# Attention's last DVE and ACT steps laid out anew, gathers tied to layer 1 in every slot, and a branch hint for PE read from a flag

## Chip, cores and metric

One core of one Trainium2 chip. The metric is the device time of one execution in microseconds, the median of the runs shown. Lower is better. TensorE is called PE in the profile, VectorE DVE, ScalarE ACT, GpSimd POOL, SyncE SP.

## What is computed

Sigmoid attention for 8 batches, 12 heads, 448 tokens of 64 values, then a mixture of 8 experts over the 3584 tokens of 768 values. Each token goes to the one expert with the largest gate logit; that expert's two layers are run on it and the result is scaled.

```python
scores = q @ k.T / sqrt(64) - log(448)
x = sigmoid(scores) @ v                      # per head; heads side by side: (3584, 768)
logits = x @ w_gate
e = argmax(logits, 1)
gate_w = softmax(logits)[e]                  # with 1e-9 in the denominator
eom = sigmoid(x @ w_output_gate)[e]
for each expert e:                           # w1: 768 x 1024, w2: 1024 x 768
    out[its tokens] = gate_w * eom * (relu(x[its tokens] @ w1[e]) @ w2[e])
```

Matmuls of the experts run as three passes on operands split in a rounded part and a rest (fp32r), which is what split() makes: a cast on ACT for the high part and a subtract on DVE for the low part.

## The kernel before

**Attention** is a loop over 168 units (L661) and two more that drain it. Seven units make a group of two head pairs, three groups make a batch. A unit issues, in this order: loads of q and k (i == 0), unit(u - 168), the routing step "places" (i == 1), scores(u), values(u - 2), the gate matmuls of the batch before (i == 3 of a batch's first group), loads of v, the routing steps "logits" (i == 6) and "counts" (i == 0), and scatters of list rows. Every engine works its own queue strictly in this order. scores (L582) are eight matmuls on PE and one sigmoid on ACT, into one of two PSUM pairs; values (L592) are eight matmuls on PE and, at i of 2, 3 and 6, the copies, adds and transposes of DVE that take a result out of PSUM (an eviction set: L600 or L604, L610, L611).

**Routing** (route, L198) is done per batch in four steps: logits (L206 to L212), counts (three sigmoids on ACT, L221 to L228 on DVE), places (L230 to L240), rows (scatters by POOL into the lists of the experts). find_run and early_table (L269) work out on DVE which expert a slot takes.

**unit(u)** (L686) counts u up to 0 at attention's end and starts the first two expert slots ahead of time, while attention still runs: early_table for slots 0 and 1, loads of the six w1 rows of slot 0 by SP (load_w) and their splits (split_w1_row, L410), list loads and copies (early_list), the gathers of slot 0's tokens by POOL (gather_rows), their transposes on DVE (turn_rows, L427) and their splits (split_rows, L433). A cast of a split stands in ACT's queue ahead of the unit's sigmoid, since unit() comes before scores().

**Slots** (slot, L504): an expert with up to 448 tokens (14 gathers of 32) or 256 tokens (8). Layer 1 is eight steps f of 18 matmuls, with a relu on ACT and a subtract on DVE for each; layer 2 is up to six blocks of 24 matmuls and, with 448 tokens, two blocks of 16 in layer2_rest (L488) after the second. Layer 2 takes three PSUM buffers in turn. Meanwhile the slot gathers the tokens of the next one (xg), turns them (turn_x) and splits them (split_x) when layer 1 is done, and loads and splits the next weights. side() is a generator that is stepped once in each f and each block of slots 0 and 1: the last batch's routing, late_table, then in turns a load of lists by SP and copies of lists by POOL (spread_lists, L364 to L367). In slot 0 (begun) two gathers are issued in each f of 0 to 6 and wait for layer 1's matmul or relu (paced); in the others all gathers are issued at the slot's start and wait for nothing of layer 1.

**Branches**: slots from the third late one on stand in nested Ifs (L783 to L787) on a register, full; then come slots of 256 tokens in nested Ifs on part (L790). Behind an If that isn't taken every engine steps its semaphore up to the count that it would have had. With these inputs five late slots of 448 tokens run, three of them inside the Ifs, and two of 256.

Of the kernel before, what the change touches and what calls it, by code (L numbers as in the profile page):

```python
# [12 lines left out]
ALU = mybir.AluOpType  # L13
# [41 lines left out]
class Kernel:  # L55
# [233 lines left out]
    def late_table(self):  # L289
        v, t = self.nc.vector, self.scratch_tiles()  # L290
        tt = v.tensor_tensor
        n = LATE_N
        keep = lambda nm, shape: self.const.tile(shape, I32, name=nm)
        sl = self.slots[:, :, 0:n].unsqueeze(3).broadcast_to([1, 2, n, E])
        left, first = t([1, E]), t([1, n])
        pos, tab = t([1, n, E]), t([1, 3, n])
        cmp, num, end = t([1, E, KT]), t([1, 2, E]), t([1, 2, E])
        base, sel = t([1, 2, E]), t([1, 2, E])
        bc = lambda a: a.unsqueeze(1).broadcast_to([1, n, E])
        self.find_run()  # L300
        tt(left, self.run, self.taken, ALU.subtract)
        tt(cmp, left.unsqueeze(2).broadcast_to([1, E, KT]), self.kts.unsqueeze(1).broadcast_to([1, E, KT]), ALU.is_gt)
        v.tensor_reduce(num[:, 0], cmp, AX.X, ALU.add)
        v.tensor_tensor_scan(end[:, 0], self.one8, num[:, 0], 0.0, ALU.mult, ALU.add)
        tt(base[:, 0], end[:, 0], num[:, 0], ALU.subtract)
        tt(sel[:, 0], self.taken, self.ebase, ALU.add)
        v.scalar_tensor_tensor(sel[:, 1], num[:, 0], float(TB), sel[:, 0], ALU.mult, ALU.add)
        v.scalar_tensor_tensor(num[:, 1], num[:, 0], float(TB), left, ALU.mult, ALU.is_lt)
        v.scalar_tensor_tensor(sel[:, 0], base[:, 0], -float(TB), sel[:, 0], ALU.mult, ALU.add)
        v.tensor_tensor_scan(end[:, 1], self.one8, num[:, 1], 0.0, ALU.mult, ALU.add)  # L310
        tt(base[:, 1], end[:, 1], num[:, 1], ALU.subtract)
        yield 1
        ohb, tb, tmb = t([1, E, E]), t([1, 3, E]), t([1, E, E])
        bb = lambda a: a.unsqueeze(1).broadcast_to([1, E, E])
        slb = self.slots[:, 0, 0:E].unsqueeze(2).broadcast_to([1, E, E])
        tt(ohb, slb, bb(base[:, 1]), ALU.is_ge)
        tt(tmb, slb, bb(end[:, 1]), ALU.is_ge)
        tt(ohb, ohb, tmb, ALU.subtract)
        tt(tmb, ohb, bb(self.ids), ALU.mult)
        v.tensor_reduce(tb[:, 0], tmb, AX.X, ALU.add)  # L320
        tt(tmb, ohb, bb(sel[:, 1]), ALU.mult)
        v.tensor_reduce(tb[:, 1], tmb, AX.X, ALU.add)
        v.tensor_reduce(tb[:, 2], ohb, AX.X, ALU.add)
        yield 1
        oh, tmp = t([1, n, E]), t([1, n, E])
        tt(oh, sl[:, 0], bc(base[:, 0]), ALU.is_ge)
        tt(tmp, sl[:, 0], bc(end[:, 0]), ALU.is_ge)
        tt(oh, oh, tmp, ALU.subtract)
        tt(tmp, oh, bc(self.ids), ALU.mult)
        v.tensor_reduce(tab[:, 0], tmp, AX.X, ALU.add)  # L330
        tt(pos, sl[:, 1], bc(sel[:, 0]), ALU.add)
        yield 1
        tt(pos, pos, oh, ALU.mult)
        v.tensor_reduce(tab[:, 1], pos, AX.X, ALU.add)
        v.tensor_reduce(tab[:, 2], oh, AX.X, ALU.add)
        v.tensor_scalar(first, self.slots[:, 0, 0:n], end[:, 0, E - 1:E], 0.0, ALU.is_equal, ALU.add)
        for i in range(3):
            v.scalar_tensor_tensor(tab[:, i], first, tb[:, i, 0:1], tab[:, i], ALU.mult, ALU.add)
        yield 1
        self.tab_l, self.tab_b, self.tot = keep("tabl", [1, 3, n]), keep("tabb", [1, 3, E]), keep("tot", [1, 2])  # L340
        v.tensor_copy(self.tab_l, tab)
        v.tensor_copy(self.tot, end[:, :, E - 1])
        v.tensor_copy(self.tab_b, tb)
        yield 1

    def take(self, key, tiles):
# [26 lines left out]
    def gather_rows(self, s, g, rows, pace=None):  # L373
# [1 line left out]
        self.paced(self.nc.gpsimd.indirect_dma_start(  # L375
            out=self.xg[:, g], out_offset=None, in_=x4,
            in_offset=bass.IndirectOffsetOnAxis(ap=s["lx"][:, g:g + 1], axis=0)), pace)

    def gather(self, s, rows=NT):
        for g in range(s["lx"].shape[1]):  # L380
            self.gather_rows(s, g, rows)

    def paced(self, i, pace):
        if pace is not None:
# [119 lines left out]
    def slot(self, cur, nxt, side=None, begun=False, hint=None):  # L504
        nx = None
        if nxt is not None:
            nx, rows, sure = nxt() if callable(nxt) else nxt
            if not begun:
                self.gather(nx, rows)
            if not sure:  # L510
                self.nc.gpsimd.drain()
        n = 32 * cur["lx"].shape[1]
        for f in range(8):
            self.layer1(f, n, begun and f == 0)
            if begun and f < 7:
                self.gather_rows(nx, 2 * f, rows, 1)
                self.gather_rows(nx, 2 * f + 1, rows, 0)
            if side is not None:
                next(side, None)
            if 1 <= f < 5:  # L520
                self.split_w2(f - 1)
                if f > 1:
                    self.load_w1(nx, f - 2)
        for k in range(3):
            self.turn_x(nx, k)
        self.split_x(nx, 0)
        self.split_x(nx, 1)
        for i in range(2 * (n // 128)):
            t = i // 2
            if hint is not None and i == 5:  # L530
                self.tc.mark_branch_hint_location(hint[0], hint=hint[1])
            self.layer2(cur, t, i % 2, self.ys[(t + (t > 0 and n % 128 > 0)) % 2])
            if i == 0:
                self.split_x(nx, 2)
            if i < 3 and nx is not None:
                self.split_w1(i)
                for k in range(i, 4 if i == 2 else i + 1):
                    self.load_w2(nx, k)
            if side is not None:
                next(side, None)  # L540
            if i == 1 and n % 128:
                self.layer2_rest(cur)
        return nx

    def attention(self, pool):
# [74 lines left out]
        def routing(at, u):  # L620
            if routes and want[0] == at:
                want[0] = next(routes[0])
                if want[0] == "rows":
                    first = u + 2 if len(rows) != B - 3 else U * NG - 20
                    rows.append((first, routes.pop(0)))
                    if routes:
                        want[0] = next(routes[0])
# [33 lines left out]
        for u in range(U * NG + LAG):  # L661
            g, i = divmod(u, U)
            if i == 0 and 0 < g < NG - 2:
                load_qk(g + 2)
            self.unit(u - U * NG)
            if i == 1:
                routing("places", u)
            if u < U * NG:
                scores(u)
            if u >= LAG:  # L670
                values(u - LAG)
            if i == 3 and g and g % GB == 0:
                gates(g // GB - 1)
            if i == 1 and 0 < g < NG - 2:
                load_v(g + 2)
            for r, name in ((6, "logits"), (0, "counts")):
                if i == r:
                    routing(name, u)
            scatters(u)
            if u == 10:  # L680
                self.init_list()
# [2 lines left out]
        return routes[-1]  # L684

    def unit(self, u):  # L686
        if u == -52:
            self.early_table(0)
            self.s0 = self.early_slot(0)
        if u == -32:  # L690
            self.early_table(1)
            self.s1 = self.early_slot(1)
        for k, a, b in ((0, -44, -42), (1, -12, -9)):
            if u == a:
                self.early_list(k, True)
            if u == b:
                self.early_list(k, False)
        for g in range(GB_):
            if u == -41 + (3 * g + 1) // 2:
                self.gather_rows(self.s0, g, ROWS_E[0], g % 2)  # L700
        for d in range(6):
            if u == (-46, -45, -43, -41, -35, -30)[d]:
                self.load_w(self.s0, self.w1, self.w1r, d, 1, 0)
            if u == (-36, -33, -30, -28, -22, -20)[d]:
                self.split_w1_row(d)
        for rows, a, b in (((0, 5), -26, -25), ((5, 10), -18, -17), ((10, GB_), -12, -11)):
            if u == a:
                self.turn_rows(self.s0, *rows)
            if u == b:
# [14 lines left out]
    def build(self, phases="abc"):  # L724
# [58 lines left out]
        with ExitStack() as ctx:  # L783
            for k in range(LATE_MIN, LATE_MAX):
                ctx.enter_context(tc.If(full > k, label=f"big{k}"))
                with tc.manual_schedule():
                    cur = self.slot(cur, late(k + 1), hint=(f"big{k + 1}", full > k + 1) if k + 1 < LATE_MAX else None)  # L787
        mid = lambda k: lambda: (self.slot_regs(self.tab_b, k, self.ltb[:, k], self.lxb[:, k], False), NT, False)
        lists = lambda k: dict(lt=self.ltb[:, k], lx=self.lxb[:, k])
        with ExitStack() as ctx:  # L790
# [39 lines left out]
```

## Time and profile before

| | before |
|---|---|
| median of 3 runs (lowest to highest) | 784.25 us (783.76 to 784.53) |
| the profiled execution | 792.04 us, its span 790.2 us |
| mean granted clock of PE in it | 0.988 |
| PE busy | 769.1 us, 97% |
| DVE busy | 398.4 us, 50% |
| ACT busy | 374.8 us, 47% |
| POOL busy | 261.7 us, 33% |

Attention takes the span from 0 to 285 us, the two early slots follow until 407.7, the five late slots of 448 tokens until 711, the two of 256 tokens until 783; then the last scatter lands. The profile is one execution, so its parts are read against its own span. Busy time is a mean over all stages: where PE has 97% over the span, it is the few stretches with less that can change. A queue's idle time carries what ended it in brackets.

### The profile page before, as it was taken

To read this page: it belongs to the slowest core of one execution; us is meant where nothing else is said; L and a number is where in the kernel's file an instruction comes from. 1 tells how busy PE (TensorE), PEld (TensorE's weight loads), DVE (VectorE), ACT (ScalarE), POOL (GpSimd) and SP (SyncE) were. 2 spreads that over 40 slices of the span, in tenths; PEclk is the share of its full clock that TensorE was granted. 3 is DMA by queue.
4 is the path that set the end of the run, shared out by engine and by line. 5 is a ranking of instruction groups with operands and counts; after the bars stand their busy time and mean duration, and the time that the engine had idled before them with its cause. 6 is when DMAs were issued, how large, how long until landed. Compare 5 with 4: busy or idle time off the path is not lost. (4 is left out here: it accounts for less than half of the span.)

```text
span 790.2 us, 14753 instructions
## 1 busy us (share of the span) xinstructions
PE 769.1 (97%) x5812; PEld 587.2 (74%) x5812; DVE 398.4 (50%) x712; ACT 374.8 (47%) x429; POOL 261.7 (33%) x374
## 2 busy tenths in 40 slices
PE   9999999999999899999999999999999999998996
PEld 4444444444333269999998999999999999998996
DVE  1373655737496549715614715615615524624564
ACT  5666666666567433424424424424424424424444
POOL 5011202112243326338736027017018117105161
PEclk9999999999999899999999999999999999999998
DMA  9475865757976355446354455254354354263541
GB/s 290 128 187 143 195 158 159 193 140 207 265 232 172 111 124 174 142 122 210 82 193 145 138 173 171 97 185 155 100 191 155 102 204 141 109 212 114 181 165 39
DMA packets 73462, 126.50 MB, mean 160 GB/s; under 512 B 15375, under 2 KB 53263, under 8 KB 73376
## 3 DMA queue, kind: packets, MB, share of 16 engines
q1 hardware_dynamic: 62768, 100.18, 42.5%
q0 software_dynamic: 9680, 24.53, 9.4%
q10 hardware_dynamic: 928, 0.69, 0.4%
q8 instruction: 49, 0.80, 0.4%
q14 instruction: 37, 0.30, 0.1%
HBM read 108.77 MB, written 23.09 MB: 167 GB/s over the span
## 5 line engine op out<-in xcount | busy, mean ns | idle before, releaser
L590 ACT ACTIVATE a<-ps,bias_s 128x896 f32<-128x896 f32 x168 | 169.0, 1008 | 92.9 <-PE ps L588 89.4
L588 PE MATMUL ps<-q,k 64*64 64x448 f32 x1344 | 161.7, 547 | 7.0 <-ACT a L590 7.0
L597 PE MATMUL ps<-a,v 64*64 64x448 f32 x1344 | 160.2, 543 | 0.7 <-DVE x L610 0.7
L449 PE MATMUL ps<-rounded 128*128 128x448 f32 (+1 forms) x432 | 151.7, 351 | 3.1 <-ACTq L783 2.8
L375 POOL DMA_INDIRECT plain<-x_dram,lxs x112 | 131.3, 1173 | 70.5 <-issue 26.7
L450 PE MATMUL ps<-rounded 128*128 128x448 f32 (+1 forms) x432 | 151.4, 350 | 0.7 <-issue 0.7
L451 PE MATMUL ps<-rounded 128*128 128x448 f32 (+1 forms) x432 | 151.3, 350 | 0.4 <-issue 0.4
L476 PE MATMUL ps<-w2h,h 128*128 128x384 f32 x400 | 133.6, 334 | 0.0
L478 PE MATMUL ps<-w2h,h 128*128 128x384 f32 x400 | 133.6, 334 | 0.0
L477 PE MATMUL ps<-w2l,h 128*128 128x384 f32 x400 | 133.6, 334 | 0.0
L462 DVE SCALAR_TENSOR_TENSOR h<-ps,h 128x384 fp32r<-128x384 f32 (+2 forms) x128 | 45.2, 390 | 165.4 <-ACT h L461 156.4
L405 DVE TENSOR_TENSOR rounded<-plain,rounded 128x2048 fp32r<-128x2048 f32 (+5 forms) x63 | 97.6, 1572 | 56.5 <-ACT rounded L404 56.4
L461 ACT ACTIVATE h<-ps 128x448 fp32r<-128x448 f32 (+1 forms) x72 | 36.8, 511 | 165.7 <-PE ps L451 132.9
L588 PEld LDWEIGHTS ps<-q,k 64*64 64x64 f32 x1344 | 51.7, 135 | 83.3 <-issue 71.0
L597 PEld LDWEIGHTS ps<-a,v 64*64 64x64 f32 x1344 | 52.6, 135 | 77.9 <-issue 73.1
L404 ACT CAST rounded<-plain 128x2048 fp32r<-128x2048 f32 (+5 forms) x63 | 83.1, 1334 | 36.3 <-DVE plain L423 26.3
L484 POOL DMA_INDIRECT out<-y,lts x28 | 30.3, 1081 | 202.9 <-ACT y L479 136.8
L449 PEld LDWEIGHTS ps<-rounded 128*128 128x128 f32 x432 | 82.2, 190 | 10.8 <-ACTq L783 3.0
L451 PEld LDWEIGHTS ps<-rounded 128*128 128x128 f32 x432 | 82.2, 190 | 7.2 <-issue 1.1
L450 PEld LDWEIGHTS ps<-rounded 128*128 128x128 f32 x432 | 82.2, 190 | 6.6 <-issue 0.5
L476 PEld LDWEIGHTS ps<-w2h,h 128*128 128x128 f32 x400 | 75.1, 188 | 0.1
L477 PEld LDWEIGHTS ps<-w2l,h 128*128 128x128 f32 x400 | 75.1, 188 | 0.1
(135 smaller groups left out, 686.2 us busy)
## 6 DMA issues: line engine op xcount, KB each, us to landing
plain<-w SPq DMA_DIRECT2D x40, 768.0 KB
plain<-w SPq DMA_DIRECT2D x27, 1024.0 KB
k<-kT SPq DMA_DIRECT2D x23, 448.0 KB
q<-qT SPq DMA_DIRECT2D x23, 448.0 KB
x_dram<-xt SPq DMA_DIRECT2D x30, 336.0 KB
v<-vm SPq DMA_DIRECT2D x24, 384.0 KB
plain<-w SPq DMA_DIRECT2D x6, 512.0 KB
plain<-x_dram,lxs POOLq DMA_INDIRECT x112
```

Source lines behind the costliest of these rows:

```text
L375: self.paced(self.nc.gpsimd.indirect_dma_start(out=self.xg[:, g], out_offset=None, in_=x4, in_offset=bass.IndirectOffsetOnAxis(ap=s["lx"][ ...
L404: self.nc.scalar.copy(hi, raw)
L405: self.nc.vector.tensor_tensor(lo, raw, r32(hi), ALU.subtract)
L449: nc.tensor.matmul(ps, wh[d][:, c], xh[:, d, 0:n], start=(d == 0), stop=False)
L450: nc.tensor.matmul(ps, wh[d][:, c], xl[:, d, 0:n], start=False, stop=False)
L451: mm = nc.tensor.matmul(ps, wl[d][:, c], xh[:, d, 0:n], start=False, stop=(d == 5))
L476: nc.tensor.matmul(ps, hh[:, f, tk], wh, start=(f == 0), stop=False)
L477: nc.tensor.matmul(ps, hh[:, f, tk], wl, start=False, stop=False)
L478: nc.tensor.matmul(ps, hl[:, f, tk], wh, start=False, stop=(f == 7))
L588: qk = nc.tensor.matmul(ps[half[h], j, 0:S], k[half[j], e, o:o + 64], q[half[j], e], start=True, stop=True)
L590: self.beat[0] = nc.scalar.activation(at[u % 3], ps[:, :, 0:S], AF.Sigmoid, bias=self.bias_s, scale=1.0 / math.sqrt(D)).ins
L597: nc.tensor.matmul(self.ps_o[e][h][half[j], 0:S], v[half[h], e, c, j], a[half[h], j], start=(i in ((0, 3 if h else 4)[e],)), stop=(i == (2 ...
```

## The change

- In the attention loop counts moves from i == 0 (behind the unit's values) to i == 2 (ahead of its scores), places from i == 1 to i == 3. The scatters of batch 5 start at unit -18 instead of -20.
- In unit(): early_table(0) from -52 to -53, early_table(1) from -32 to -22; the first list load from -44 to -45; slot 0's gathers two units later; the w1 rows' loads from -46 ... -30 to -50 ... -36 and their splits from -36 ... -20 to -44 ... -28; turns of rows from -26, -18, -12 to -25, -19, -8 and their splits from -25, -17, -11 to -23, -17, -6.
- In slot(): every slot now issues its gathers two in each f, behind layer 1's step, tied to its matmul and relu; the drain comes behind the last pair.
- late_table keeps a flag per late slot, more (one DVE operation); in the Ifs the branch hint is a register that PE alone loads from it, and it is set for PE alone. Before, the hint was the comparison full > k + 1 for all engines.

```diff
+        self.more = keep("more", [1, n])
...
+        v.tensor_scalar(self.more, self.slots[:, 0, 0:n], end[:, 0, E - 1:E], 0.0, ALU.is_lt, ALU.add)
...
-    def gather(self, s, rows=NT):
-        for g in range(s["lx"].shape[1]):
-            self.gather_rows(s, g, rows)
...
-            if not begun:
-                self.gather(nx, rows)
-            if not sure:
-                self.nc.gpsimd.drain()
+            last = -(-nx["lx"].shape[1] // 2) - 1
...
-            if begun and f < 7:
+            if nx is not None and f <= last:
                 self.gather_rows(nx, 2 * f, rows, 1)
                 self.gather_rows(nx, 2 * f + 1, rows, 0)
+                if f == last and not sure:
+                    self.nc.gpsimd.drain()
...
             if hint is not None and i == 5:
-                self.tc.mark_branch_hint_location(hint[0], hint=hint[1])
+                more = self.nc.values_load(self.more[0:1, hint[1]:hint[1] + 1], engines=[ET.PE], min_val=0, max_val=1)
+                self.tc.mark_branch_hint_location(hint[0], hint=more, engines=[ET.PE])
...
-                    first = u + 2 if len(rows) != B - 3 else U * NG - 20
+                    first = u + 2 if len(rows) != B - 3 else U * NG - 18
...
-            if i == 1:
-                routing("places", u)
+            for r, name in ((2, "counts"), (3, "places")):
+                if i == r:
+                    routing(name, u)
...
-            for r, name in ((6, "logits"), (0, "counts")):
-                if i == r:
-                    routing(name, u)
+            if i == 6:
+                routing("logits", u)
...
-        if u == -52:
+        if u == -53:
             self.early_table(0)
...
-        if u == -32:
+        if u == -22:
             self.early_table(1)
...
-        for k, a, b in ((0, -44, -42), (1, -12, -9)):
+        for k, a, b in ((0, -45, -42), (1, -12, -9)):
...
-            if u == -41 + (3 * g + 1) // 2:
+            if u == -39 + (3 * g + 1) // 2:
                 self.gather_rows(self.s0, g, ROWS_E[0], g % 2)
-        for d in range(6):
-            if u == (-46, -45, -43, -41, -35, -30)[d]:
+        for d, (a, b) in enumerate(((-50, -44), (-49, -42), (-46, -40), (-43, -37), (-38, -30), (-36, -28))):
+            if u == a:
                 self.load_w(self.s0, self.w1, self.w1r, d, 1, 0)
-            if u == (-36, -33, -30, -28, -22, -20)[d]:
+            if u == b:
                 self.split_w1_row(d)
-        for rows, a, b in (((0, 5), -26, -25), ((5, 10), -18, -17), ((10, GB_), -12, -11)):
+        for rows, a, b in (((0, 5), -25, -23), ((5, 10), -19, -17), ((10, GB_), -8, -6)):
...
-                    cur = self.slot(cur, late(k + 1), hint=(f"big{k + 1}", full > k + 1) if k + 1 < LATE_MAX else None)
+                    cur = self.slot(cur, late(k + 1), hint=(f"big{k + 1}", k + 1) if k + 1 < LATE_MAX else None)
```

## Rows read from the trace of the kernel before

**Rows 1.** Busy time by stretch: us, engines' busy us (instructions), PE's granted clock, DMA share, GB/s
```profile
200.00:290.00 90.00, 81.56 (x854) 34.59 (x854) 55.40 (x125) 53.26 (x60) 28.92 (x57) 0.94 0.61 179
290.00:700.00 410.00, 408.62 (x2200) 389.01 (x2177) 196.09 (x282) 154.65 (x182) 168.49 (x204) 1.00 0.47 153
```

**Rows 2.** Waits of PE: what waited, for whom, us, times, longest
```profile
PE ps L642 <- issue: 1.2, 3, 0.8
PE ps L597 <- DVE x L610: 0.7, 1, 0.7
```

**Rows 3.** Timeline of PE: start, us, line, tiles [idle before, releaser]
```profile
238.47 1.13 PE L588 MATMUL ps<-q,k 64*64 64x448 f32 x8 [2.66 <-ACT a L590]
...
243.22 0.93 PE L588 MATMUL ps<-q,k 64*64 64x448 f32 x8
...
244.72 0.93 PE L588 MATMUL ps<-q,k 64*64 64x448 f32 x8
...
267.59 1.77 PE L588 MATMUL ps<-q,k 64*64 64x448 f32 x8 [3.94 <-ACT a L590]
...
273.47 0.92 PE L588 MATMUL ps<-q,k 64*64 64x448 f32 x8
```

**Rows 4.** Timeline of ACT, the cast at the first hole
```profile
236.51 0.99 ACT L404 CAST rounded<-plain 128x960 fp32r<-128x960 f32 x1 [4.25 <-DVE plain L429]
```

**Rows 5.** Timeline of DVE, first operations of its steps, 212 to 266 us
```profile
212.20 1.23 DVE L646 TENSOR_TENSOR num<-num,ps 64x224 f32<-64x224 f32 x3
...
227.21 0.19 DVE L262 STREAM_TRANSPOSE turned<-last 32x32 f32<-32x32 f32 x1
...
229.50 0.60 DVE L600 COPY xh<-ps 128x448 f32<-128x448 f32 x1
...
235.34 1.14 DVE L429 STREAM_TRANSPOSE plain<-plain 128x960 f32<-128x960 f32 x1
...
253.06 1.15 DVE L405 TENSOR_TENSOR rounded<-plain,rounded 128x960 fp32r<-128x960 f32 x1
...
256.20 0.36 DVE L206 STREAM_TRANSPOSE lg<-num 64x224 f32<-64x224 f32 x1
...
257.79 0.40 DVE L221 STREAM_TRANSPOSE turn<-oh 64x224 f32<-64x224 f32 x1
...
260.21 0.40 DVE L230 STREAM_TRANSPOSE turn<-num 64x224 f32<-64x224 f32 x1
...
262.96 0.61 DVE L604 COPY xh<-ps 128x448 f32<-128x448 f32 x1
...
264.83 0.94 DVE L429 STREAM_TRANSPOSE plain<-plain 128x768 f32<-128x768 f32 x1
```

**Rows 6.** Timeline of all engines in slot 1, 380 to 394 us
```profile
380.77 0.22 POOL L364 COPY lxs<-hb 32x28 int32<-32x28 int32 x1
...
382.49 3.10 DVE L423 STREAM_TRANSPOSE plain<-plain 128x896 f32<-128x896 f32 x3 [3.88 <-DMA plain<-x_dram,lxs]
...
384.24 0.19 POOL L365 COPY ltb<-hb 32x12 int32<-32x12 int32 x1
...
385.49 0.57 ACT L479 ACTIVATE y<-ps,lts 128x384 f32<-128x384 f32 x1
...
388.24 0.33 PE L498 MATMUL ps<-w2h,h 128*128 128x384 f32 x1
...
391.02 0.33 PE L476 MATMUL ps<-w2h,h 128*128 128x384 f32 x1
...
393.23 1.13 DVE L501 SCALAR_TENSOR_TENSOR y<-ps,lts,y 64x384 f32<-64x384 f32 x2
```

**Rows 7.** The If's line L783: ns min/median/max, first and last start; who waited
```profile
L783 PEldq COMPARE_BRANCH  x5: 65/92/5317, 527.0 to 713.3; - x5
...
L783 ACTq EVENT_SEMAPHORE  x1: 17/17/17, 713.6 to 713.6; - x1
...
  PE ps L449: 2.8, 1
```

## The prediction

> **What bounds the kernel now.** I read the stretches first [rows 1]. From 290 to 700 us TensorE is busy 408.62 of 410 us at full clock, and the 1.38 us that lack end on nothing that the profile shows: little can be won there, much lost. It is idle 8.44 us in 200 to 290, at a granted clock of 0.94. So attention's end is the place, and besides it the one gap behind the If chain, at 711. The waits of TensorE name the small causes: an eviction on DVE (0.7 us) and the gate matmuls (1.2 us "issue", no cause shown) [rows 2], and the way out of the If chain (2.8 us) [rows 7].
>
> The two large holes stand in TensorE's own row of time [rows 3]: 2.66 us before 238.47 and 3.94 us before 267.59, both ended by the sigmoid of L590. [...] **Cost of the two holes: 2.66 + 1.74 + 3.94 + 2.87 = 11.2 us; with the 0.7 us eviction 11.9.**
>
> Why does the sigmoid come late? In ACT's queue a cast of split_rows stands ahead of it and waits for DVE's turn_rows, 4.25 us at the first hole [rows 4]. DVE isn't slow, it is overbooked. Prices [rows 5]: logits 257.79 - 256.20 = 1.59, counts 260.21 - 257.79 = 2.42, places 262.96 - 260.21 = 2.75, one eviction set (copy, add, transpose) 264.83 - 262.96 = 1.87, early_table 229.50 - 227.21 = 2.29, a split's subtract 1.15, taken for a w1 row too, turns 1.14 and 0.94. First hole: the gate sums end at about 213.4 (212.20 + 1.23). Queued before the end of the first turn: four sets 7.48, the route 6.76, early_table(1) 2.29, four w1 rows 4.60, the turn 1.14, in all 22.3: it ends at 235.7 (236.48 in the trace). Second hole: from 253.06, when the gate sums are over: the subtract of rows 5 to 9 1.15, two sets 3.74, the route 6.76, the turn 0.94 = 12.6, so 265.7 (265.77 in the trace). The bookkeeping closes within 0.8 us, so I use it for the new layout.
>
> **The change: DVE and ACT before the end (units count steps of 1.504 us back from the end).** First stretch: early_table(1) goes to unit -22, one of the four w1 subtracts is done before the gates (units -44 to -28 instead of -36 to -20), and the cast waits two units behind the turn (-25, -23) instead of one. Left ahead of the turn's end: 7.48 + 6.76 + 3.45 + 1.14 = 18.8, so about 232.2 on the old time line; unit -23 comes to ACT at about 234.3. The hole closes with 2 us to spare. So does the 0.7 us eviction, which came late behind early_table(1). Second stretch: turn at -8, cast at -6. Ahead: 1.15 + three sets 5.61 + 6.76 + 0.94 = 14.5, so 267.5, and up to 1.7 us more where DVE must wait for TensorE between the sets; ACT wants the cast at 268.6. That is a wait of 0 to 0.7, and ACT has some 0.9 us between the end of one sigmoid and the scores that need it, so 0 to 1 us is left of the hole; I take 0.3. Counts two units later only put three short sigmoids ahead of scores, whose input has long been there. **Gain 11.9 - 0.3 = 11.6 us.**
>
> Queues passed: SP's list load at -45 now waits for a scatter of unit -46, before for one of -48; behind it stand w1 row 3, a q/k load and the x stores, none due for six units. early_table(1) at -22 holds SP's register load, with a q/k load and w2 loads behind, due 14 units later. Each w1 row now has 6 to 8 units (at least 9.0 us) from load to cast, 10 to 13 before. At the 179 GB/s of the stretch [rows 1] the 512 KB of a row take 2.9 us alone, and 10.4 us with a group's q, k and v (1.34 MB) ahead, so between hidden and 1.4 us late; no cast of before waited for a load, I take hidden. The gathers move two units and end at -19, eleven ahead of their last turn. The gate matmuls' 1.2 us has no shown cause: between kept and gone (0 to 1.2 gain), I keep it.
>
> **Gathers tied in all slots.** Slot 0 had this order already and TensorE did not wait in it [rows 1]. A slot from 2 on has the same pace, so 0. POOL's drain moves behind the gathers; behind it stand scatters that wait for layer 2 anyway. Mid slots are bound by POOL's own 1.2 us a gather: 0. **Slot 1 is the exception.** There POOL ends the gathers late, just ahead of the copies at 380.77, and DVE's turn at 382.49 waited 3.88 us for them [rows 6]. In the old order the list copies of side() (L364 to L367) come behind all fourteen gathers. In the new one side() steps between them, so the copies of two calls run ahead of the last two to four gathers: 380.77 to 384.43, 3.66 us [rows 6]. The turn moves by that, and with it ACT's first y eviction, 385.49 to 389.15, ending at 389.7. Layer 2 has three PSUM buffers; the fourth block (second half of layer2_rest) begins at 388.24 and needs it: TensorE stands 1.4 us. The next block, at 391.02, needs the second eviction, and the one behind that DVE's L501 at 393.23 + 3.66 = 396.9: some 0.4 each. **Cost 2.2 us** (0 if the copies fall into gaps; 3.9 if the clock falls too, by the smaller loss of rows 3; gaps of 0.7 did not lower it, so I leave it out).
>
> **Branch hints by flag.** On the way out PE's compare-and-branch takes 5317 ns, with a median of 92 over the five [rows 7], and no instruction of L531 is in the trace: the hint of before did nothing. [...] The first matmul behind the If waits for ACT: the 2.8 us are put down to ACTq L783, whose semaphore step comes at 713.6 [rows 7], and ACT gets no hint. So TensorE can't start earlier than it did, and I take 0. The flag load on PE is one register load in each of three slots, ahead of 24 matmuls already queued; the extra DVE operation is one of 0.2 us in slot 0: 0. [...]
>
> **Sum.** 790.2 - 11.6 + 2.2 = 780.8 us of span, -9.4. The profiled run was 792.04 us, the median of the plain runs 784.25; I take the same difference off that: **774.8 us**.
>
> **Rivals.** (1) *No price in slot 1, or the gate matmuls heal*: -9.4 - 2.2 - 1.2, 771.4. For it: copies are short, and the side work depends on SP's list loads, whose time can shift. Against: POOL is strictly in order. (2) *The exit heals*: the hint frees TensorE at once, 2.8 idle and, by the smaller loss of rows 3, 1.7 of half clock less: 770.3. For it: PE's branch is the longest item there. Against: the wait is ended by ACT. (3) *DVE and ACT stay tighter than the rows say*: DVE 10% slower would leave some 2.5 us, or one hole with its clock loss, 4.4: 777.3 to 779.2. For it: stretch two has no more than 1 us to spare. (4) *Slower: w1 rows land after their cast's turn.* The six casts now stand in ACT's queue 9.0 to 12 us behind their loads, each ahead of a sigmoid. A row landing at 13 us holds ACT 4 us: 3.1 idle behind the 0.9 slack and, by the smaller loss of rows 3, 1.74: 4.8 a row. From two such rows on the gain is gone; with four it is 784.25 - 9.4 + 19.4 = 794. Against it: the 10.4 us bound needs a whole group's loads ahead. (5) *The work only moves*: the holes open elsewhere, or aren't there without the profiler; 784.
>
> **How the numbers follow.** Forecast 0.50, (1) 0.20, (2) 0.07, (3) 0.11, (4) 0.06, (5) 0.06. About 0.2% (1.6 us) can be told from no change. Faster: 0.50 + 0.20 + 0.07 + 0.11 = 0.88; same 0.06; slower 0.06. The range takes in forecast, (1), (2) and most of (3): 769.5 to 779.5; (4), (5) stay outside.
>
> **What would show it.** No idle of over 1 us on TensorE in the last 60 units, granted clock 1.00 there, no ACT cast waiting over 1 us for L429 or a load; in slot 1 copies ahead of the last gathers, the turn some 3.6 us later and TensorE idle 1 to 2 us ahead of layer2_rest's second half; behind the If the wait still ended by ACT while PE's branch is short. Wrong if ACT waits for w1 loads, if slots 2 to 6 show idle TensorE, or if TensorE starts behind the If before ACT's step.

## The result and the profile after

| | after | before |
|---|---|---|
| median (lowest to highest) | 775.12 us (773.43 to 776.75, 4 runs) | 784.25 us (783.76 to 784.53, 4 runs) |
| ratio, 95% interval | 0.9884 (0.9858 to 0.991) | |
| the profiled execution, its span | 773.99 us, 772.1 us | 792.04 us, 790.2 us |
| mean granted clock of PE | 0.997 | 0.988 |
| PE busy | 760.7 us, 99% | 769.1 us, 97% |

Forecast was 774.8, 9.4 us less than before; it became 9.1 less. The span of the profiled execution fell by 18.1, twice as much: the profiled execution of before lay 7.8 us above its median, that of after 1.1 below. The point-by-point part shows where the extra time lay.

Two stretches of after, by busy time (columns as in [rows 1]):

```profile
200.00:275.00 75.00, 75.00 (x879) 32.50 (x869) 54.81 (x124) 52.65 (x60) 30.38 (x58) 1.00 0.68 206
290.00:700.00 410.00, 407.12 (x2175) 388.62 (x2174) 186.62 (x252) 151.36 (x176) 165.19 (x199) 1.00 0.47 154
```

At attention's end, where [rows 1] lacked 8.44 us at a clock of 0.94, nothing is idle and the clock is 1.00. In the second stretch 2.88 us are idle; 2.66 of them are the way out of the If chain, which has moved into this window. All waits of TensorE over 0.1 us:

```profile
PE ps L447 <- ACTq L781: 2.7, 1, 2.7
PE ps L657 <- DVE rounded L650: 1.2, 1, 1.2
PE ps L586 <- ACT a L588: 0.4, 1, 0.4
PE ps L474 <- DVE y L499: 0.2, 1, 0.2
```

The first is the way out of the Ifs (2.8 in [rows 7]), the second and third are at the start of the kernel. The eviction and the gate matmuls of [rows 2] are gone. The three casts of slot 0's rows in ACT's queue, which answer [rows 4]:

```profile
232.59 0.98 ACT L402 CAST rounded<-plain 128x960 fp32r<-128x960 f32 x1
241.61 0.98 ACT L402 CAST rounded<-plain 128x960 fp32r<-128x960 f32 x1
260.29 0.83 ACT L402 CAST rounded<-plain 128x768 fp32r<-128x768 f32 x1 [0.59 <-DVE plain L427]
```

Only the last waits for its turn, 0.59 us (forecast: 0 to 0.7), and ACT's slack takes that up.

Below, stages are compared by the starts of their first matmuls. Attention with the 20 matmuls ahead of it, from 1.24 us to slot 0's first matmul, takes 284.35 us in the profile of before, 268.54 in that of after; layer 2 of slot 1 takes 30.51 before and 31.54 after; layer 1 of slot 2 takes 31.62 before and 29.75 after; every other slot's layers take the same within 0.1 us up to the way out of the Ifs.

### The profile page after: what moved, and what is told of

It is laid out like the page before. It is cut to its first block, busy times and chain, and to the rows that moved or that the text cites. A ratio compares the mean times of both kernels' runs of the same rounds, so it can differ in the third digit from the quotient of the medians.

```text
span 772.1 us, 14844 instructions
## 1 busy us (share of the span) xinstructions
PE 760.7 (99%) x5812; PEld 583.6 (76%) x5812; DVE 398.2 (52%) x713; ACT 374.2 (48%) x429; POOL 265.6 (34%) x374
## 5 line engine op out<-in xcount | busy, mean ns | idle before, releaser
L377 POOL DMA_INDIRECT plain<-x_dram,lxs x112 | 138.6, 1237 | 73.0 <-ACT h L459 25.4
L586 PE MATMUL ps<-q,k 64*64 64x448 f32 x1344 | 157.3, 539 | 0.4 <-ACT a L588 0.4
L595 PE MATMUL ps<-a,v 64*64 64x448 f32 x1344 | 156.3, 536 | 0.0
```

The costliest lines, as they stand in the source:

```text
L377: self.paced(self.nc.gpsimd.indirect_dma_start(out=self.xg[:, g], out_offset=None, in_=x4, in_offset=bass.IndirectOffsetOnAxis(ap=s["lx"][ ...
L586: qk = nc.tensor.matmul(ps[half[h], j, 0:S], k[half[j], e, o:o + 64], q[half[j], e], start=True, stop=True)
L595: nc.tensor.matmul(self.ps_o[e][h][half[j], 0:S], v[half[h], e, c, j], a[half[h], j], start=(i in ((0, 3 if h else 4)[e],)), stop=(i == (2 ...
```

## The experiments

Kernels that were timed together, on one chip, share their runs of the kernel before. Two of these groups ran on chips on which the kernel before takes 788 and 789 us instead of 784, so times are compared only within a group, and stages by their profiles. "Half clock" is a granted clock of 0.50 in a window, as behind the Ifs in after_again (697 to 701 us, below), full clock one of 1.00.

### The parts alone

```diff
 attention_only: before, with all hunks of attention(), unit() and the -18 of the scatters
 tied_only:      before, with the hunks of gather() and of the gathers in slot()
 hint_only:      before, with self.more and the two lines of the hint
```

> The kernel before with the new attention layout alone (gathers and branch hint as before). Theory: the whole gain sits here. 11.9 us of holes less 0.3 left: 784.25 - 11.6 = 772.7, and TensorE runs from 200 us to attention's end with under 0.5 us idle; slot 1 has no idle, the gap behind the If stays near 2.8 us. Rival: part of the changed kernel's gain comes from the hint or the ties (a way out of the If without half clock is worth 1.4): then this one stands at 774 to 775, above the changed kernel less its slot-1 price.

> The kernel before with the gathers tied in every slot alone. Theory, with the changed kernel's profile: three short stops of TensorE in slot 1, 1.0 us in all (the turn comes some 2.2 us later within its slot), nothing in the other slots: 785.3. By the price of the prediction (2.2) it would be 786.4. Rival: the ties cost nothing or help later slots: 784.2 or less.

> The kernel before with the flag hint on TensorE alone. Theory: TensorE's branch on the way out gets shorter (3 us instead of 5.3) but ACT's semaphore step still ends the wait, so 784.2, within 0.3, and 2.7 us idle behind the If. Rival: it ends the half clock behind the If (1.4) or the wait (2.8): 780 to 782.8.

> The changed kernel once more, for its spread and a second profile. Theory: runs fall in two groups, near 773.7 and near 776.5, 2.8 us apart, at granted clocks of 0.997 and 0.993; a profile in the second group shows where: half clock behind the If (1.4) and a stop at the gate matmuls or in a slot of layer 1. Rival: one group and a slow drift, with no place of its own.

| timed together | median (range), runs | ratio to before (784.25), interval |
|---|---|---|
| attention_only | 772.26 (772.01 to 774.63), 4 | 0.9852 (0.9835 to 0.9868) |
| tied_only | 786.8 (786.04 to 790.62), 9 | 1.0034 (1.0019 to 1.005) |
| hint_only | 784.73 (783.19 to 787.31), 11 | 1.0006 (0.9996 to 1.0017) |
| after_again | 776.18 (773.88 to 777.02), 4 | 0.9883 (0.9866 to 0.99) |

**The whole gain is the attention layout's; the ties cost, the hint alone does nothing that can be measured.** attention_only beats both kernels. Its layer 2 of slot 1 takes 30.51 us, and TensorE waits nowhere but at the start and behind the If. It lies 2.9 us below the median of after and 3.9 below that of after_again. The stops in slot 1, measured below, are 1.0 of that. The rest is about the size of the half clock behind the Ifs, which after_again's profile has and attention_only's has not; whether the ties or the hint make it more frequent, no run here shows.

hint_only leaves attention as it was and so gives a second look at the kernel before, with a span (783.0 us) near the median. TensorE's timeline at its holes, to be laid beside [rows 3]:

```profile
229.66 0.98 PE L600 MATMUL ps<-a,v 64*64 64x448 f32 x8 [0.68 <-DVE x L613]
236.31 0.98 PE L591 MATMUL ps<-q,k 64*64 64x448 f32 x8 [2.66 <-ACT a L593]
237.11 0.93 PE L600 MATMUL ps<-a,v 64*64 64x448 f32 x8
...
263.05 1.77 PE L591 MATMUL ps<-q,k 64*64 64x448 f32 x8 [4.01 <-ACT a L593]
264.60 1.72 PE L600 MATMUL ps<-a,v 64*64 64x448 f32 x8
266.09 0.98 PE L591 MATMUL ps<-q,k 64*64 64x448 f32 x8
```

Idle times are the same, the clock isn't. Behind the first hole the next block starts 0.80 us later, against 0.75 at a granted clock of 1.00 (before, 232 to 234 us): full clock. Behind the second two blocks take 3.04 us instead of 1.50, then full clock again. The gate matmuls have no "issue". Attention takes 278.54 us here, 10.0 more than in after and 5.8 less than in the profiled execution of before.

tied_only's slot 1, TensorE and POOL's second gather:

```profile
383.62 0.44 PE L494 MATMUL ps<-w2h,h 128*128 128x384 f32 x1 [1.08 <-ACT y L475]
391.40 0.44 PE L472 MATMUL ps<-w2h,h 128*128 128x384 f32 x1 [0.20 <-DVE y L497]
```
```profile
354.95 2.46 POOL L375 DMA_INDIRECT plain<-x_dram,lxs  x1 [0.30 <-ACT w2h L400]
```

Its layer 2 takes 32.74 us, 2.23 more than before: the price that the prediction put on it (2.2), at the places it named. The turn starts 8.74 us into layer 2 instead of 5.35, so 3.39 later (predicted 3.66), and the three stops with the slower matmul behind each cost 1.36, 0.33 and 0.48 (predicted 1.4, 0.4 and 0.4). The run's own theory, 1.0 us and 785.3, missed; 786.4 by the prediction's price came closer. In after the price is 1.03. The next part says why.

after_again has the same stages as after but one: the first layer 1 behind the Ifs takes 20.04 us instead of 17.38. Windows behind that gap, first of after, then of after_again:

```profile
697.00:699.00 2.00, 1.92 (x16) 1.92 (x17) 0.00 (x0) 0.00 (x0) 0.00 (x0) 1.00 0.51 198
699.00:701.00 2.00, 2.00 (x19) 2.00 (x18) 0.43 (x1) 0.38 (x1) 0.00 (x0) 1.00 0.02 7
```
```profile
697.00:699.00 2.00, 1.74 (x8) 1.74 (x9) 0.00 (x0) 0.00 (x0) 0.62 (x1) 0.50 0.45 177
699.00:701.00 2.00, 2.00 (x11) 2.00 (x11) 0.00 (x0) 0.00 (x0) 0.00 (x0) 0.50 0.09 32
```

The gap is 2.7 us in both; in one the granted clock stays at 1.00, in the other it is 0.50. That is 2.66 us, and the eight runs of this kernel lie at 773.4 to 774.0 (three) and at 775.7 to 777.0 (five). Nothing else in the two profiles differs by over 0.2 us; of the expectation, the half clock behind the If is there, with 2.66 instead of 1.4, and the stop at a gate matmul or in a slot is not. The clock accounts for the two profiles, not for every run: the run of 775.68 us has the mean clock of the faster ones, 0.997, and no trace of it was kept. The median of after, 775.12, lies between two runs on either side; over all eight runs it is 775.96.

### Slot 1: what the ties cost

```diff
 slot1_untied (on after):  -cur = self.slot(cur, late(0), sd)
                           +cur = self.slot(cur, late(0), sd, tied=False)   # all gathers at the slot's start
 pool_two_copies_more (on after), in lists(), behind the second spread_lists:
                           +for _ in range(2): nc.gpsimd.tensor_copy(lx[96:128, o + a:o + b], lq[:, :, :, 3])
```

> The changed kernel with slot 1 alone put back to gathers at the slot's start. Theory: the list copies run behind the gathers again, the turn of slot 1 comes 3.4 us earlier within its slot, layer 2 of slot 1 takes 30.5 us instead of 31.5, the time falls by 1.0: 774.1 by the medians so far (775.1). Rival: the ties aren't what stops TensorE there (DVE's splits are), then layer 2 keeps 31.5 and the time 775.1.

> The changed kernel with one list copy of POOL made twice more (same data, some 0.4 us of POOL in all) just ahead of slot 1's first gather. Theory: slot 1's price hangs on whether its second gather starts before or after the first of DVE's four w2 subtracts, 13.29 us into the slot. In the changed kernel it starts at 13.19 and takes 0.98; here it would start at 13.5, take 2.4 to 2.5, end 0.82 behind the subtract, and slot 1's layer 2 takes 32.7 to 32.8 us instead of 31.5: 1.2 us lost to 0.4 us of POOL. Rival: the gathers just move by 0.4 and layer 2 by 0.4 or less; or the slow gathers have nothing to do with the subtracts.

slot1_untied: 776.21 us (775.46 to 776.89) where before takes 788.47 (785.58 to 792.32): 0.9842 (0.9812 to 0.9872). No after ran beside it, so its time can't be set against 775.1; its stage can: layer 2 of slot 1 takes 30.51 us. Untying this one slot takes the whole price away. The copies ahead of the last gathers are how the ties cost it, as POOL's row in after shows:

```profile
357.75 0.95 POOL L377 DMA_INDIRECT plain<-x_dram,lxs  x1 [0.30 <-issue]
358.75 0.23 POOL L366 COPY lxs<-hb 32x28 int32<-32x28 int32 x1
...
360.98 0.98 POOL L377 DMA_INDIRECT plain<-x_dram,lxs  x1 [0.15 <-issue]
362.26 0.95 POOL L377 DMA_INDIRECT plain<-x_dram,lxs  x1 [0.30 <-ACT h L459]
363.25 0.22 POOL L366 COPY lxb<-hb 32x24 int32<-32x24 int32 x1
...
364.94 0.98 POOL L377 DMA_INDIRECT plain<-x_dram,lxs  x1 [0.15 <-issue]
```

Gathers elsewhere in this row that nothing holds start 1.25 us apart; the first block of copies puts 1.98 more between two of them, the second 1.43, together 3.41.

Now the size. The turn starts 5.35 us into layer 2 of slot 1 in the kernel before, 7.55 in after: 2.2 later, not 3.66.

```profile
368.94 3.10 DVE L421 STREAM_TRANSPOSE plain<-plain 128x896 f32<-128x896 f32 x3 [6.08 <-DMA plain<-x_dram,lxs]
```

But in attention_only, whose gathers aren't tied, it starts 4.08 in; against that the ties moved it by 3.47. The new attention layout by itself brought it 1.27 forward. In after, POOL's second and third gather, and the second of DVE's four subtracts of the w2 splits (the expectation above calls it the first; the first starts at 341.21, ahead of all gathers):

```profile
344.83 0.98 POOL L377 DMA_INDIRECT plain<-x_dram,lxs  x1 [0.30 <-issue]
346.11 1.40 POOL L377 DMA_INDIRECT plain<-x_dram,lxs  x1 [0.30 <-issue]
```
```profile
344.93 1.76 DVE L403 TENSOR_TENSOR w2l<-plain,w2h 128x1536 fp32r<-128x1536 f32 x1 [0.67 <-ACT w2h L402]
```

The gather of 344.83 starts 0.10 us before the subtract and takes 0.98. In the kernel before, in tied_only and in pool_two_copies_more the same gather starts 0.1 to 0.3 behind the subtract's start and takes 2.3 to 2.5. Here is the last of them:

```profile
344.96 2.33 POOL L377 DMA_INDIRECT plain<-x_dram,lxs  x1 [0.30 <-ACT w2h L402]
```
```profile
344.69 1.76 DVE L403 TENSOR_TENSOR w2l<-plain,w2h 128x1536 fp32r<-128x1536 f32 x1 [0.67 <-ACT w2h L402]
```
```profile
373.44 0.44 PE L496 MATMUL ps<-w2h,h 128*128 128x384 f32 x1 [1.02 <-ACT y L477]
```

The w1_loads_late run below, with after's slots, shows it once more: its gather starts 0.13 behind, takes 2.48, and layer 2 takes 32.81.

In pool_two_copies_more, 0.4 us more of POOL's work made layer 2 of slot 1 32.64 us long instead of 31.54, 1.1 more (forecast 1.2; the 776.48 us of the run, 0.9905 (0.9889 to 0.9922) of a before of 784.09, also hold 1.5 of half clock behind the Ifs). **The price of the ties is 1.0 or some 2.2 us, by the side of the subtract's start on which one gather falls.** In after itself it falls on the cheap side, and TensorE's three short stops stand where 1.4, 0.4 and 0.4 had been forecast:

```profile
361.39 0.34 PE L474 MATMUL ps<-w2h,h 128*128 128x384 f32 x1
...
372.32 0.34 PE L497 MATMUL ps<-w2l,h 128*128 128x384 f32 x1
372.55 0.44 PE L496 MATMUL ps<-w2h,h 128*128 128x384 f32 x1
...
375.29 0.34 PE L497 MATMUL ps<-w2l,h 128*128 128x384 f32 x1
375.67 0.44 PE L474 MATMUL ps<-w2h,h 128*128 128x384 f32 x1
...
380.32 0.44 PE L474 MATMUL ps<-w2h,h 128*128 128x384 f32 x1 [0.18 <-DVE y L499]
...
392.93 0.36 PE L447 MATMUL ps<-rounded 128*128 128x448 f32 x1
```

Starts are 0.173 apart elsewhere; here 0.23, 0.38 and (from 379.80) 0.52, and the matmul behind each stop takes 0.1 more: 0.17, 0.31 and 0.45, together 0.93 of the 1.03.

### The order in ACT's queue, and the rest of the layout

```diff
 cast_next_unit (on after): (((0, 5), -25, -24), ((5, 10), -19, -18), ((10, GB_), -8, -7))
 turns_only (on before):    (((0, 5), -25, -23), ((5, 10), -19, -17), ((10, GB_), -8, -6))
 w1_loads_late (on after):  ((-46, -44), (-44, -42), (-42, -40), (-39, -37), (-32, -30), (-30, -28))
 after_third:               after
```

> The changed kernel with the three casts one unit behind their turns instead of two (units -24, -18, -7). Theory: the last cast comes to ACT 1.5 us earlier and waits 2.1 us for DVE's turn instead of 0.6; of such a wait TensorE felt all but 0.83 in the kernel before (4.84 waited, 4.01 idle), so 1.3 us idle, and 1.5 more if the clock halves: 776.4 to 777.9; the second cast waits about 1.2 and costs 0 to 0.4, the first nothing. Rival: the order in ACT's queue doesn't matter, DVE's load alone does: 775.1, no idle.

> The kernel before with the units of the turns and of their casts alone changed; counts, places, tables, w1 loads and splits as before. Theory by the bookkeeping: at the first place the turn still ends behind early_table and four w1 subtracts, the cast two units behind it waits 1.2 us and costs 0 to 0.4, the late eviction (1.2 us with the slow block around it) stays, the second hole closes: 784.25 - 10.0 + 1.2 to 1.6 = 775.5 to 775.9 (with gathers untied, so without slot 1's price). Rival: the other moves are needed to close the holes: 778 to 781; or they are worth nothing: 774.2.

> The changed kernel again, as the base of the two beside it. Theory: 773.4 to 777.0 as before, attention 268.5 us, slot 1's layer 2 31.5, and behind the If 17.4, 18.8 or 20.0 us for the first layer 1, by how long the half clock lasts. On a chip where the kernel before takes 788 instead of 784, some stops of TensorE near 200 us and at the gate matmuls come on top, about 1.5 us.

> The changed kernel with the six w1 row loads two units (3.0 us) ahead of their casts instead of six to eight. Theory of the slower rival: a cast that waits for its load holds the sigmoid behind it. The first row took 3.8 us from issue to landing with the queues free, so it is 0.8 late, within ACT's slack; a row that stands behind a group's q, k and v takes up to 10.4, so 7.4 late and some 6.5 of idle and 1.5 of half clock. With one to three such rows: 8 to 24 us slower than the base, all between 196 and 230 us. Rival: loads are hidden even so, or land in time: within 1 us of the base.

cast_next_unit took 778.7 us (776.16 to 780.51), turns_only 777.25 (776.93 to 778.03), timed beside slot1_untied (776.21). ACT's second and third cast and TensorE in cast_next_unit:

```profile
243.22 0.99 ACT L402 CAST rounded<-plain 128x960 fp32r<-128x960 f32 x1 [1.18 <-DVE plain L427]
262.08 0.83 ACT L402 CAST rounded<-plain 128x768 fp32r<-128x768 f32 x1 [2.09 <-DVE plain L427]
```
```profile
263.87 0.98 PE L586 MATMUL ps<-q,k 64*64 64x448 f32 x8 [1.26 <-ACT a L588]
```

Waits of 1.18 and 2.09 against 1.2 and 2.1 forecast, idle 1.26 against 1.3, at full clock. One unit in ACT's queue is worth that much; DVE's load is the same in both. turns_only closes both holes with the units of turns and casts alone: its three casts wait 0.20, 0.87 and nothing. What it keeps is the late eviction, and "issue" stops at the gate matmuls (0.53 us idle in all):

```profile
231.22 0.98 PE L597 MATMUL ps<-a,v 64*64 64x448 f32 x8 [0.68 <-DVE x L610]
```

The other moves (tables, w1, counts, places) are worth that eviction, 1.2 us with the slow block ahead of it. The medians, 777.25 against 776.21 of slot1_untied, which has no slot-1 price either, do not measure it: in their profiles attention is 2.5 us longer in turns_only, 1.3 of it at the eviction and 0.9 at the second gate block, and slot1_untied loses 1.5 by half clock behind the Ifs. turns_only is 11.2 below the before of its own chip, where 8.4 to 8.8 were forecast; no profile of before is known to come from that chip, so what else it won there stays open.

after_third took 777.32 us (775.54 to 778.52) and w1_loads_late 796.18 (793.81 to 797.79) beside it, 18.9 more, where before takes 789.06 (786.48 to 791.99). Four of the five casts that waited for a row in w1_loads_late (the fifth, at 241.32, waited 2.89 us), and the longest stop of TensorE:

```profile
201.82 1.04 ACT L402 CAST rounded<-plain 128x1024 fp32r<-128x1024 f32 x1 [1.49 <-DMA plain<-w]
207.49 1.04 ACT L402 CAST rounded<-plain 128x1024 fp32r<-128x1024 f32 x1 [2.82 <-DMA plain<-w]
211.67 1.04 ACT L402 CAST rounded<-plain 128x1024 fp32r<-128x1024 f32 x1 [1.33 <-DMA plain<-w]
225.66 1.04 ACT L402 CAST rounded<-plain 128x1024 fp32r<-128x1024 f32 x1 [9.58 <-DMA plain<-w]
```
```profile
227.66 1.77 PE L586 MATMUL ps<-q,k 64*64 64x448 f32 x8 [8.96 <-ACT a L588]
```

So the slower rival is a real mechanism: a row that stands behind a group's loads held ACT for 9.58 us. With the change's own gap of six to eight units no cast of any profile waited for a w1 row for more than 0.10 us (attention_only, once).

### The way out of the Ifs

```diff
 act_hint (on after):               engines=[ET.PE] -> [ET.PE, ET.Activation], for the flag's load and the hint
 hint_two_engines_early (on after): the same, and  -if hint is not None and i == 5:  +... i == 0:
```

> The changed kernel with the flag loaded and the hint set on ACT too. Theory: ACT's 2.5 us between its compare-and-branch and its semaphore step behind the If is what holds TensorE; with the branch foreseen TensorE is next held by its own way out, at 695.3 instead of 697.1: the gap falls from 2.8 to about 1.0 us, and 1.8 us are gained (773.3), up to 2.7 more where the half clock behind the gap goes with it. [...]

> The changed kernel with the hint on TensorE and ACT, and placed ahead of layer 2's first block instead of its sixth, some 20 us before the branch instead of 3.7. [...] Rival: lead doesn't matter, ACT's 2.8 us stay, the gap stays 2.7 to 2.9, the time is the base's.

act_hint took 777.65 us (774.79 to 780.74), timed beside slot1_untied and without an after beside it; its gap is 2.9 us. hint_two_engines_early took 778.2 (776.82 to 779.52) beside after_third (777.32). No gain shows. The If's line in attention_only (the old hint, of which no instruction is in the trace), after, and hint_two_engines_early:

```profile
L783 PEldq COMPARE_BRANCH  x5: 65/92/5257, 508.6 to 694.8; - x5
  PE ps L449: 2.8, 1
```
```profile
L781 PEldq COMPARE_BRANCH  x5: 65/92/3095, 510.4 to 694.8; - x5
L781 ACTq EVENT_SEMAPHORE  x1: 17/17/17, 697.0 to 697.0; - x1
  PE ps L447: 2.7, 1
```
```profile
L781 PEldq COMPARE_BRANCH  x5: 65/92/378, 512.4 to 696.8; - x5
L781 ACTq EVENT_SEMAPHORE  x2: 17/17/17, 699.0 to 699.1; - x2
  PE ps L447: 2.7, 1
```

TensorE's branch falls from 5.3 to 3.1 and to 0.38 us; its wait doesn't move. ACT's semaphore step comes 2.54 us behind ACT's own compare-and-branch in after, 2.80 in act_hint and 2.57 in hint_two_engines_early, though in both of the latter ACT has run the hint instruction (3.6 and 26.7 us ahead). ACT holds TensorE, as forecast; act_hint's theory, that with a hint on ACT the gap falls to about 1.0 us, did not come true. Of what hint_two_engines_early was built for, TensorE's branch under 0.5 us came; ACT's step within 0.6 us of its branch, a gap of 1 us or less and 1.8 us gained did not. What these 2.5 us are stays open.

## Why the prediction was right, point by point

**Attention's end: right place, a size that came out 1.6 too large.** The holes close as the bookkeeping said: the turns are in time, the last cast waits 0.59, TensorE runs through. Forecast gain 11.6; against hint_only, whose execution stands for the median, it is 278.54 - 268.54 = 10.0. The term that was mis-sized is the clock. The sum's 1.74 and 2.87 are the 4.75 and 5.88 us of the four blocks behind each hole in [rows 3] less 3.01, twice the 1.50 of two blocks at full clock; that one execution has granted clocks of 0.62 (238.5 to 243.0 us) and 0.51 (267.6 to 273.4) there. No run shows the two as a cost that stays: in hint_only the 1.74 are 0 and the 2.87 are 1.54. The eviction and the two idle times were in turn worth 1.2, 2.9 and 4.2 with the slower matmuls around them, a little more than 0.7, 2.66 and 3.94. In all 1.2 + 2.9 + 4.2 + 1.5 = 9.8 of the 10.0. Idle times taken from one execution held; what the clock does behind them did not. attention_only's median, 12.0 below before, looks like the forecast 11.6, but that is luck: some 1.5 of it lies behind the Ifs, where its profile has no half clock and hint_only's has.

**Gate matmuls: kept was right for the median, though the profile lost them.** The "issue" of [rows 2] isn't in hint_only, tied_only or after. It is in the profiled execution of before, with other extras: laid block by block against hint_only, that execution loses 2.7 us around the two gate blocks, 2.9 by more half clock behind the holes, 1.9 in slot 2's layer 1 (where the 1.38 us lie that [rows 1] lack between 290 and 700) and 0.2 in small pieces, 7.7 in all, and it lay 7.8 above the median. To take that difference off at the end was what kept the forecast right. What stops the gate matmuls stays open. turns_only's profile, from a chip where before takes 785.6 to 792.3 us, has such stops too; the profile of before may come from such a chip, which no record says.

**w1 rows, queues, rival (4): right.** No cast of after waits for a row; w1_loads_late shows what the price would have been.

**Slots from 2 on, mids: right, 0.** Slots 2 to 6 take the same times tied and untied.

**Slot 1: mechanism right, 2.2 mis-sized to 1.03 in this kernel.** The places were right, and for the old attention layout the size too (2.23). The failing step is the turn's delay, 3.66, taken against the kernel before's turn: the new layout starts POOL's gathers 0.37 us earlier in the slot, one gather escapes DVE's subtract, and the turn comes 2.2 later instead. So the sign that the prediction named, 1 to 2 us idle ahead of layer2_rest's second half, shows in tied_only and not in after, where that stop costs 0.17.

**Branch: right.** The old hint left no instruction, the new one shortens TensorE's branch (5.3 us before, 3.1 in after), ACT ends the wait (2.8 and 2.7), gain 0 (hint_only 1.0006, 0.9996 to 1.0017).

**The sum** is -11.6 + 2.2 = -9.4 against -10.0 + 1.03 = -9.0: two errors of 1.6 and 1.2 us with opposite signs. That the forecast came within 0.3 us of the median is luck; what the runs bear out is the mechanism of each term, with the two sizes off. The median of 775.12 is itself the middle of two shorter and two longer runs; by all eight runs the gain is 8.3. Of the rivals, (1) names the chance that slot 1 is free; attention_only, where it is, stands at 772.26. What could not have been known from one trace is how far the clock falls behind the Ifs, 0 to 2.66 us from execution to execution; the sum has no term for it.

## What to carry to other kernels

When an in-order engine carries the critical sigmoid, put a helper step that waits for another engine two units behind its producer, and add up that producer's queue: the last cast's wait came out at 0.59 where 0 to 0.7 had been added up. Size idle gaps from one trace, but size the clock's loss behind them from several, and lay the traced execution beside the median before summing. Test a bundle's parts alone: here one part held the whole gain and another took at least 1.0 us of it back.

## What the runs showed of the hardware that was not expected

**Of 202 gathers that began beside a w2 subtract of DVE, 196 ended 0.81 to 0.84 us behind its end.** In the traces of before, after, tied_only, attention_only, slot1_untied and w1_loads_late, 202 gathers began with over 0.3 us left of a w2 subtract (two fp32 inputs in SBUF). Six of them, begun within 0.04 us of the subtract's start, took 0.95 us like free ones; the other 196 took 2.16 at the median, 2.54 at most. The 225 that began while no DVE operation ran took 0.95 at the median, none over 1.02; beside the relu's subtract, one of whose inputs is in PSUM, it was 0.95 too. The two subtracts differ in length as well (1.76 us against some 0.4), so what in the w2 subtract holds the gather is not shown.

**The hint's lead and TensorE's branch.** The branch out of the Ifs took 5.3 us without a hint that works (before, attention_only), 3.1 to 3.8 with the hint 3.7 us ahead (after, after_third, act_hint), 0.38 with it 30.7 us ahead (hint_two_engines_early). TensorE's wait behind it was 2.7 to 3.0 us in all of them.

**Stops with no cause shown.** On the two other chips, where before took 788 to 789 us, the five profiles with after's tables and w1 loads (slot1_untied, act_hint, cast_next_unit, after_third, hint_two_engines_early) lose 1.1 to 1.3 us at 197 to 204 us, by stops and the slower blocks behind them, and 0.6 around the first gate block; after, after_again, attention_only and pool_two_copies_more don't have these; no run here separates their cause.
